# Retention and hard-swish MLP on one core: the heads' first values loaded as fp16 in 1 KB runs through GpSimd's queue and put in order by TensorE

## Chip, cores and metric

The kernel runs on one core of a Trainium2 chip. The metric is device time in microseconds, the median of several executions. A core has TensorE (PE, matrix products; PEld is its weight load), VectorE (DVE), ScalarE (ACT), GpSimd (POOL) and SyncE (SP). PE writes only to PSUM; the other engines take results from there back to SBUF. Transfers are issued by SP, ACT or POOL and run on 16 DMA engines that all three share. A transfer that changes the type on its way (fp32 to fp16) is issued from POOL here.

## The reference

Retention over 8 batches, 8 heads, 576 positions and a head dimension of 64, then a two-layer MLP on the 4608 tokens:

```python
scores = scale * np.matmul(q, k.transpose(0, 1, 3, 2))       # scale = 1/8
gamma = 1.0 - 2.0 ** (-5.0 - np.arange(H))                   # one decay per head
Dmat = np.where(rel >= 0, gamma[:, None, None] ** rel, 0.0)  # rel = row - column
attn = np.matmul(scores * Dmat, v)                           # (8, 8, 576, 64)
x = attn.transpose(0, 2, 1, 3).reshape(4608, 512)
h = x @ w_in                                                 # 512 -> 2048
out = (h * np.clip(h + 3.0, 0.0, 6.0) / 6.0) @ w_out         # 2048 -> 512
```

All inputs and the output are fp32. The products run in fp16 with sums in fp32.

## The kernel before, in words

**Blocks.** Each batch's 576 positions are cut into 64 first positions (the "heads" of the sequences, TL = 64) and one block of 512. The eight groups of 64 together make block 0, the eight blocks of 512 are blocks 1 to 8. Block 0 is computed directly, without a carried state; blocks 1 to 8 go in chunks of 128 positions that carry a state from chunk to chunk. For each block the MLP runs in two stages: 16 `up` units (`up_steps`, each four products of 128x512, then an ACT and a DVE instruction), and the `down` products. `down` of a block is interleaved with `up` of the next by plans written out by hand (`go`, and the tables behind it). The order on every engine is the order in which the program names the instructions.

**The start, on which the change works** (from `indices()` on, L714 to L784). For each of four pairs of heads (i = 0 to 3) the kernel loads k and q of the first 64 positions with `load_half`: 128 partitions hold (batch, r), each with 4 neighbouring positions times 64 values, so that each run in memory is 1 KB. Pair 0 of k goes by SP and ACT, all q by SP and ACT; k of pairs 1 to 3 goes by POOL, cast to fp16 on the way. `turn_heads` turns them with products against `by_chunk`, a permuted identity, so that the positions come out in order. `scores_heads` makes the scores, DVE multiplies them with a mask (L458). `inner_heads(i)` multiplies the masked scores with the values `vh` of pair i and writes a quarter of `xT0`, the input of the first `up` units. `idle_products` are products whose results nobody reads.

**The values of block 0.** `load_values` (L431, called twice) loads them by SP behind all of q, 128 partitions by position in the chunk, in runs of 64 values (256 bytes), fp32, into `vf`. `values_heads(c)` (L438) casts chunk c to fp16 into `vh`; ACT does chunks 0 and 1, POOL chunks 2 and 3. Each chunk holds all heads, so `inner_heads(0)` needs all four.

**The weights.** `win_piece(n)` (L642) loads a quarter of w_in (1 MB in fp32) as fp16 by POOL's queue; piece 0 goes in two halves, behind the last q (`queries`); pieces 2 and 3 and the four `wout_piece` (L650) are named after the first four units (L773 to L775), so that on POOL they stand behind its two casts of the values. Units 4n to 4n+3 use piece n. `decays()` (L120, POOL, then one ACT Exp) and two smaller tables stand on POOL behind the weights. `fetch(8, wout[2])` (L779) makes SP wait until the third w_out transfer has landed, and then loads the chunks of block 1.

**Queues.** A queue has eight semaphores for its transfers, used in turn, and in the built program a transfer that takes a semaphore again first waits, on the issuing engine, for the transfer that had it, eight before.

**Buffers.** PSUM tiles of tag `pp` have six buffers and take scores, `inner_heads` and `up` results in turn; tag `st` has two and takes the results of `turn_heads` and later of `down`. `ws[1]` to `ws[4]` hold sums of w_out later, and lend their space to early tables.

Of the kernel before, what the change touches and what calls it, by code (L numbers as in the profile page):

```python
# [12 lines left out]
FP32 = mybir.dt.float32  # L13
# [8 lines left out]
def kernel(  # L22
# [9 lines left out]
    nc = tc.nc  # L32
# [3 lines left out]
    P = 128  # L36
# [353 lines left out]
    def load_half(i, nm, e, queue, behind=None):  # L390

        if nm not in hd.setdefault(i, {}):
            if queue is nc.gpsimd:
                hd[i][nm] = heads16(i, nm)
            else:
                f = half_tile(io, "fq", i, FP32, "hq", bufs=2) if nm == "q" else io.tile(
                    [P, H * D], FP32, tag=f"f{nm}", name=f"h{nm}{i}")
                hd[i][nm] = f.rearrange("p (e j d) -> p e j d", e=2, j=NJ)
        d = queue.dma_start(hd[i][nm][:, e].rearrange("p j d -> p (j d)"),  # L399
                            dict(q=q, k=k, v=v)[nm][:, 2 * i + e, 0:TL, :].rearrange("b (r j) d -> r b (j d)", j=NJ))  # L400
        if behind is not None:
            after(d, behind)
        return d
# [6 lines left out]
    def cast_heads(i, nm, copy):  # L410
        t = heads16(i, nm)
        copy(t, hd[i][nm])
        hd[i][nm] = t

    def turn_heads(i, nm, copy):
        pt = psum.tile([P, NJ, P], FP32, tag="st", bufs=2, name=f"hpt{nm}{i}")
        for j in range(NJ):
            for e in range(2):
                nc.tensor.matmul(pt[e * D:e * D + D, j, :], hd[i][nm][:, e, j, :], by_chunk, start=True, stop=True,
                                 skip_group_check=True)  # L420
        t = half_tile(work, "qT", i, FP16, "hqT", bufs=3) if nm == "q" else work.tile(
            [P, H * D], FP16, tag="kT", bufs=4, name=f"hkT{i}")
        if nm == "q":
            copy(t.rearrange("p (x j r) -> p x j r", j=NJ, r=RP), pt.rearrange("p j (x r) -> p x j r", r=RP))
        else:
            copy(t.rearrange("p (x r j) -> p x r j", j=NJ, r=RP), pt.rearrange("p j (x r) -> p x r j", r=RP))
        hd[i][nm + "T"] = t.rearrange("p (c y) -> p c y", c=NCB)

    vf = gp.tile([P, NCB, H * D], FP32, tag="g", bufs=4, name="hv")

    def load_values(c, n):  # L431

        for e in range(2):
            b = c + NCB * e
            nc.sync.dma_start(vf[rows(e), c:c + n].rearrange("p c (h d) -> p (c h) d", h=H),  # L435
                              v[b:b + n, :, 0:TL, :].rearrange("b h s d -> s (b h) d"))

    def values_heads(c, copy):  # L438
        copy(vh[:, c].rearrange("p i e d -> p (i e d)"), vf[:, c])

    def keys_heads(i):
        pk = psum.tile([P, NCB, 2, D], FP32, tag="pp", name=f"hpk{i}")
# [199 lines left out]
    def win_piece(n, parts=1, behind=None):  # L642
        a, b = pieces_in[n]
        for i in range(parts):
            cc = slice(NP // parts * i, NP // parts * (i + 1))
            d = nc.gpsimd.dma_start(win16[n][:, cc], win_v[:, cc, BLK * a:BLK * b])
            if behind is not None:
                after(d, behind)
# [62 lines left out]
    with tc.manual_schedule(engines={ENG.PE, ENG.DVE, ENG.Pool, ENG.Activation, ENG.SP}):  # L711
        sp, act, pool = nc.sync, nc.scalar, nc.gpsimd
        on_act, on_dve = nc.scalar.copy, nc.vector.tensor_copy
        indices()  # L714
        for nm in ("k", "q"):
            landed = load_half(0, nm, 0, sp)
            keys = landed if nm == "k" else keys
            load_half(0, nm, 1, act)
        nc.scalar.activation(warm, half, ACTF.Exp)
        load_half(1, "q", 0, sp)  # L720
        load_half(1, "q", 1, act)
        for i in (2, 3):
            for e in range(2):
                queries = load_half(i, "q", e, sp, keys)
        load_values(0, 2)
        load_values(2, 2)
        for i in (1, 2, 3):
            for e in range(2):
                load_half(i, "k", e, pool, None if i == 1 else keys)
        win_piece(0, 2, queries)  # L730
        win_piece(1)
        distances()
        idle_products(5)
        mask_of_heads(0)
        cast_heads(0, "k", on_dve)
        turn_heads(0, "k", on_act)
        mask_of_heads(1)
        idle_products(4)
        cast_heads(0, "q", on_dve)
        mask_of_heads(2)  # L740
        turn_heads(0, "q", on_act)
        cast_heads(1, "q", on_dve)
        turn_heads(1, "k", on_act)
        turn_heads(1, "q", on_act)
        cast_heads(2, "q", on_dve)
        scores_heads(0)
        mask_of_heads(3)
        idle_products(1)
        turn_heads(2, "k", on_act)
        turn_heads(2, "q", on_act)  # L750
        cast_heads(3, "q", on_dve)
        scores_heads(1)
        idle_products(1)
        turn_heads(3, "k", on_act)
        turn_heads(3, "q", on_act)
        scores_heads(2)
        scores_heads(3)
        for c in range(NCB):
            values_heads(c, on_act if c < 2 else pool.tensor_copy)
        idle_products(2)  # L760
        inner_heads(0, on_act)
        inner_heads(1, on_act)
        inner_heads(2, on_dve)
        first = [up_steps(0, u) for u in range(4)]
        for dmc in range(3):
            for unit in first:
                next(unit)
            if dmc == 1:
                inner_heads(3, on_act)
        for unit in first:  # L770
            for _ in unit:
                pass
        for n in (2, 3):  # L773
            win_piece(n)
        wout = [wout_piece(pc) for pc in (0, 2, 1, 3)]  # L775
        decays()
        mask_of_chunk()
        decays_of_chunk()
        fetch(8, wout[2])  # L779
        for u in range(4, NFC):  # L780
            up_unit(0, u)
        weight_sums(3)
        weight_sums(1, 2, 4)
        down = down_plain(0)  # L784
        go("k0 D4 k1 D4 +1 k2 D4 +1 k3 D6 h0 D2 c4 h1 D3 h2 D3 h3 D3 D4 c5 t4 D5 a4 s4 u4 D5 z4 t5 c6 D4 "
           "x4 a5 s5 i4 u5 z5 D5 t6 x5 D2 i5 D4 L2 c7 a6 s6 u6 L3 z6 D1 t7 L3 x6 a7 s7 i6 u7 D1 L1 z7 L2 c8 L1 D2 x7 D1 i7 t8 D3 "
           "R3 c9 R3 a8 s8 u8 R2 t9 z8 R4 c10 x8 a9 s9 i8 u9 U1 z9 c11 t10 U3",
           1, down)
        down = down_plain(1)
        go("c12 D6 x9 a10 s10 i9 u10 z10 D2 t11 c13 +1 D7 x10 a11 s11 i10 u11 z11 c14 +2 D8 x11 D2 i11 t12 +1 D3 +1 D3 "  # L790
           "a12 s12 u12 t13 D2 c15 D2 z12 +1 D4 x12 a13 s13 i12 u13 z13 D1",
           down=down)
        go("U1 D3 t14 U1 D2 U1 U1 D2 x13 a14 s14 i13 u14 z14 o1 c16 U1 D2 U1 D2 t15 U1 D2 U1 D2 +1 U1 x14 a15 s15 i14 u15 z15 "
           "c17 D2 U1 D2 +1 U1 D2 +1 U1 D2 x15 +1 U1 i15 t16 c18 +1 U1 D2 t17 U1 U1",
           2, down)
        for kb in range(2, NB):
# [60 lines left out]
```

## Time and profile before

| | |
|---|---|
| three runs | 302.41, 302.86 (median), 303.16 us |
| profiled execution: span from first to last instruction | 301.3 us |
| between that span and the median of the runs | 1.56 us |
| PE busy, DVE, ACT, POOL | 95%, 70%, 64%, 42% of the span |
| DMA | 48.37 MB, mean 161 GB/s |

The profiled execution is one execution taken by the hardware's profiler. Only its span is listed, not a time of its own; what lies around the span is taken to be the 1.56 us between it and the median. In the profile a line is an engine, a source line of the kernel (L153 is the helper of all the 128-row products), the operation and the tiles' names. "x16" is a count. Where an idle time is given in brackets, it lies just ahead of the instruction, with what ended it. Start times are counted from the start of the span.

### The profile page before, as it was taken

What the parts mean: (1) busy time and instruction counts of PE and PEld (TensorE: products, weight loads), DVE (VectorE), ACT (ScalarE), POOL (GpSimd) and SP (SyncE); (2) the same over time, 40 slices, a digit from 0 to 9 for tenths busy, and PEclk for the clock granted to TensorE, in tenths of its full rate; (3) what the DMA queues carried; (4) which work ended last, traced back from release to release, by engine and by line L of the source; (5) the groups of instructions that cost most, each with busy time, mean ns of one, the idle gap of its engine ahead of it and who ended that gap; (6) DMA issues with size and microseconds to landing.
All of it is one profiled execution on the core that took longest, in us unless ns stands there. A gap on an engine that the chain in (4) does not pass through costs nothing.

```text
span 301.3 us, 12401 instructions
## 1 busy us (share of the span) xinstructions
PE 287.0 (95%) x5450; PEld 220.7 (73%) x5450; DVE 211.8 (70%) x382; ACT 193.8 (64%) x360; POOL 128.0 (42%) x163
## 2 busy tenths in 40 slices
PE   6839999989999999999999999999999999999995
PEld 2527866778655657888887877887878977787895
DVE  4713854678886777888968696779768776657554
ACT  5715875799876786866767667657766675555420
POOL 5247028553773750808641964195238003100510
PEclk9978999999999999999999999999999999999999
DMA  6999999998999989998999999979928100210114
GB/s 151 204 153 200 214 215 217 214 227 194 175 200 156 244 183 200 193 198 238 207 246 178 196 200 216 182 140 269 136 25 143 72 2 2 104 40 2 72 72 139
DMA packets 122549, 48.37 MB, mean 161 GB/s; under 512 B 96384, under 2 KB 117888, under 8 KB 122496
## 3 DMA queue, kind: packets, MB, share of 16 engines
q1 hardware_dynamic: 118496, 42.61, 72.0%
q0 software_dynamic: 3568, 4.59, 9.0%
q8 instruction: 42, 0.69, 1.0%
q10 hardware_dynamic: 432, 0.39, 0.4%
q14 instruction: 11, 0.09, 0.2%
HBM read 36.70 MB, written 9.44 MB: 153 GB/s over the span
## 4 chain that ended last, share of the span: by engine, by line
PE 89%; DMA 5%; ACT 2%; SPq 1%; DVE 1%; issue 0%; POOL 0%; ACTq 0%; POOLq 0%
PE ph L153 42%; PE pm L153 29%; PE pd L153 9%; PE po L231 4%; DMA hv<-in_v_dram 3%; PE pa L231 3%; DMA hq<-in_q_dram 2%; PE pu L231 1%; SPq L435 1%; PE ptk L153 1%; PE ptq L153 1%; SPq L399 1%; PE hpo L467 0%; ACT u L498 0%; DVE qT L211 0%; DVE g L500 0%
## 5 line engine op out<-in xcount | busy, mean ns | idle before, releaser
L153 PE MATMUL ph<-xT,win 128*64 128x512 f16 (+1 forms) x1248 | 146.3, 367 | 0.7 <-ACT xT L369 0.4
L500 DVE SCALAR_TENSOR_TENSOR g<-u,ph 128x512 f16<-128x512 f32 (+1 forms) x156 | 98.6, 644 | 53.4 <-ACT u L498 52.8
L498 ACT ACTIVATE u<-ph,half 128x512 f32<-128x512 f32 (+1 forms) x156 | 100.1, 659 | 42.6 <-PE ph L153 40.2
L153 PEld LDWEIGHTS <-win 128*64 128x64 f16 x1248 | 85.8, 136 | 26.1 <-issue 2.0
L153 PEld LDWEIGHTS <-g 128*64 128x64 f16 x928 | 51.7, 110 | 14.4 <-issue 0.4
L153 PEld LDWEIGHTS <-s 128*64 128x64 f16 x896 | 50.3, 110 | 8.3 <-issue 0.5
L317 POOL TENSOR_TENSOR z<-z,gpow 128x256 f32<-128x256 f32 x24 | 15.8, 657 | 70.6 <-DVE z L316 49.6
L153 PE MATMUL pm<-ws,s 128*64 128x256 f16 x672 | 45.7, 273 | 0.0
L192 POOL TENSOR_TENSOR q<-fq,dec 128x512 f16<-128x512 f32 x32 | 36.7, 1167 | 0.0
L369 ACT CAST xT<-po 128x256 f16<-128x256 f32 (+1 forms) x44 | 22.5, 583 | 21.5 <-PE po L231 21.5
L195 POOL TENSOR_TENSOR v<-fv,dec 128x512 f16<-128x512 f32 x32 | 35.4, 1111 | 1.9 <-DMA fv<-in_v_dram 1.9
L153 PE MATMUL pd<-wout,g 128*64 128x512 f16 x256 | 34.9, 382 | 0.1
L579 POOL TENSOR_TENSOR u<-u,p 128x512 f32<-128x512 f32 x7 | 8.9, 1271 | 60.4 <-ACT u L619 54.1
L153 PE MATMUL pm<-wout,g 128*64 128x256 f16 x448 | 31.1, 273 | 0.0
L266 DVE TENSOR_TENSOR a<-pa,mask 128x256 f16<-128x256 f32 (+1 forms) x44 | 21.9, 540 | 7.9 <-PE pa L231 4.2
L188 ACT CAST k<-fk 128x512 f16<-128x512 f32 x32 | 19.8, 620 | 0.0
L515 DVE TENSOR_TENSOR s<-g 128x1024 f16<-128x1024 f16 x28 | 19.3, 691 | 0.2
L323 ACT CAST z<-z 128x512 f16<-128x512 f32 x24 | 14.8, 619 | 5.2 <-DVE z L313 5.0
L153 PE MATMUL pm<-ws,g 128*64 128x256 f16 x224 | 16.7, 274 | 0.0
L153 PE MATMUL pm<-wout,s 128*64 128x256 f16 x224 | 16.3, 273 | 0.1
L515 DVE TENSOR_TENSOR s<-g,s 128x1024 f16<-128x1024 f16 x14 | 13.1, 934 | 0.0
L231 PE MATMUL po<-qT,z 64*64 64x64 f16 x512 | 12.5, 198 | 0.4 <-ACT z L326 0.3
(101 smaller groups left out, 252.6 us busy)
## 6 DMA issues: line engine op xcount, KB each, us to landing
fk<-in_k_dram SPq DMA_DIRECT2D x32, 256.0 KB, 4.6
fq<-in_q_dram SPq DMA_DIRECT2D x16, 512.0 KB, 6.1
fv<-in_v_dram SPq DMA_DIRECT2D x32, 256.0 KB, 5.9
out_dram<-o SPq DMA_DIRECT2D x14, 512.0 KB, 4.0
wout<-in_moe_w_out_dram POOLq DMA_DIRECT2D x4, 512.0 KB, 12.8
out_dram<-o SPq DMA_DIRECT2D x7, 256.0 KB, 5.1
win<-in_moe_w_in_dram POOLq DMA_DIRECT2D x3, 512.0 KB, 7.4
hv<-in_v_dram SPq DMA_DIRECT2D x4, 256.0 KB, 7.1
```

Of the source, the lines that this page charges most:

```text
L153: nc.tensor.matmul(out[r], lhs[:, r], rhs, skip_group_check=True, **flags)
L188: nc.scalar.copy(by_head(k16), in_rows(st[c]["fk"]))
L192: nc.gpsimd.tensor_tensor(by_head(q16[:, e]), in_rows(st[c]["fq"][:, :, e, :]), in_rows(dd[:, 2 + e, 0:H, :]), ALU.mult)
L195: nc.gpsimd.tensor_tensor(v16, st[c]["fv"], dd[:, 1, H:2 * H, :], ALU.mult)
L231: return lambda: nc.tensor.matmul(*args, skip_group_check=True, **flags)
L266: nc.vector.tensor_tensor(a16[:, a, 0:n].rearrange("p x i q -> p (x i) q"), pa[a].rearrange("p x i q -> p (x i) q"), m, ALU.mult)
L317: nc.gpsimd.tensor_tensor(new, new, decay, ALU.mult)
L323: nc.scalar.copy(z16, zs[c])
L369: nc.scalar.copy(xt[:, s], po[s].rearrange("p x n (e r) -> p x n e r", e=2))
L498: nc.scalar.activation(uu[:, 0:n], ph[:, 0:n], ACTF.Relu, bias=half, scale=1.0 / 6.0)
L500: nc.vector.scalar_tensor_tensor(out=g[:, hf, ths, jr, :], in0=by_half(uu), scalar=1.0, in1=by_half(ph), op0=ALU.min, op1=ALU.mult)
L515: nc.vector.tensor_tensor(*pend.popleft())
```

## The change

1. `load_values(i)` now loads the values of pair i by POOL's queue (L439 of the kernel after), cast to fp16 on the way, in the layout of q and k: two transfers of 128 partitions x 256 elements for each pair, 1 KB runs. The fp32 tile `vf` and its four SP transfers are gone.
2. `picks()`: four selection matrices in `pick` (the space of `ws[2]`), set to zero by POOL (128x2048 fp16, between k of pair 1 and k of pair 2) and filled by four DVE copies of `by_chunk` behind the first cast of k.
3. `values_heads(i)` now is 16 products on PE (four chunks x four j), 32 matmuls of 128 columns, and one copy from PSUM to `vh`: ACT for pairs 0, 1 and 3, DVE for pair 2. The four calls stand between `scores_heads(2)` and `inner_heads(2)`.
4. All weights are issued by POOL right behind the values, in the order w_in 0 to 3, w_out 0, 2, 1, 3. The wait for `queries` is gone.
5. `inner_heads(1)` is copied out by DVE instead of ACT. Two idle products (four matmuls) behind the scores are gone.

```diff
-    vf = gp.tile([P, NCB, H * D], FP32, tag="g", bufs=4, name="hv")
-    def load_values(c, n):
-        for e in range(2):
-            b = c + NCB * e
-            nc.sync.dma_start(vf[rows(e), c:c + n].rearrange("p c (h d) -> p (c h) d", h=H),
-                              v[b:b + n, :, 0:TL, :].rearrange("b h s d -> s (b h) d"))
-    def values_heads(c, copy):
-        copy(vh[:, c].rearrange("p i e d -> p (i e d)"), vf[:, c])
+    pick = ws[2].rearrange("p j n -> p (j n)").rearrange("p (j c m) -> p j c m", j=NJ, c=NCB)
+    def picks():
+        for j in range(NJ):
+            nc.vector.tensor_copy(pick[:, j].rearrange("p c (x j) -> p (c x) j", j=NJ)[:, :, j], by_chunk)
+    def load_values(i, behind=None):
+        t = heads16(i, "v")
+        for e in range(2):
+            d = nc.gpsimd.dma_start(t[:, e].rearrange("p j d -> p (j d)"),
+                                    v[:, 2 * i + e, 0:TL, :].rearrange("b (r j) d -> r b (j d)", j=NJ))
...
+    def values_heads(i, copy):
+        pv = psum.tile([P, NCB, 2, D], FP32, tag="st", bufs=2, name=f"hpv{i}")
+        for c in range(NCB):
+            for j in range(NJ):
+                product(pv[:, c], pick[:, j, c, :], hd[i]["v"][:, :, j, :], start=(j == 0), stop=(j == NJ - 1))
+        copy(vh[:, :, i], pv)
...
-        load_values(0, 2)
-        load_values(2, 2)
         for i in (1, 2, 3):
             for e in range(2):
                 load_half(i, "k", e, pool, None if i == 1 else keys)
-        win_piece(0, 2, queries)
-        win_piece(1)
+            if i == 1:
+                nc.gpsimd.memset(pick, 0.0)
+        for i in range(NP):
+            load_values(i)
+        win_piece(0, 2)
+        for n in (1, 2, 3):
+            win_piece(n)
+        wout = [wout_piece(pc) for pc in (0, 2, 1, 3)]
...
         cast_heads(0, "k", on_dve)
+        picks()
...
         scores_heads(2)
+        values_heads(0, on_act)
         scores_heads(3)
-        for c in range(NCB):
-            values_heads(c, on_act if c < 2 else pool.tensor_copy)
-        idle_products(2)
+        values_heads(1, on_act)
         inner_heads(0, on_act)
-        inner_heads(1, on_act)
+        values_heads(2, on_dve)
+        inner_heads(1, on_dve)
+        values_heads(3, on_act)
         inner_heads(2, on_dve)
...
-        for n in (2, 3):
-            win_piece(n)
-        wout = [wout_piece(pc) for pc in (0, 2, 1, 3)]
         decays()
```

More of the change, by code (lines that the diff above doesn't have):

```diff
@@ L427, in turn_heads @@
         hd[i][nm + "T"] = t.rearrange("p (c y) -> p c y", c=NCB)
-    vf = gp.tile([P, NCB, H * D], FP32, tag="g", bufs=4, name="hv")
-    def load_values(c, n):
-        for e in range(2):
-            b = c + NCB * e
-            nc.sync.dma_start(vf[rows(e), c:c + n].rearrange("p c (h d) -> p (c h) d", h=H),
-                              v[b:b + n, :, 0:TL, :].rearrange("b h s d -> s (b h) d"))
-    def values_heads(c, copy):
-        copy(vh[:, c].rearrange("p i e d -> p (i e d)"), vf[:, c])
+    pick = ws[2].rearrange("p j n -> p (j n)").rearrange("p (j c m) -> p j c m", j=NJ, c=NCB)
[4 more added lines that the diff above has]
+        t = heads16(i, "v")
+        for e in range(2):
+            d = nc.gpsimd.dma_start(t[:, e].rearrange("p j d -> p (j d)"),
+                                    v[:, 2 * i + e, 0:TL, :].rearrange("b (r j) d -> r b (j d)", j=NJ))
+            if behind is not None:
+                after(d, behind)
+        hd.setdefault(i, {})["v"] = t
+    def values_heads(i, copy):
[4 more added lines that the diff above has]
+        copy(vh[:, :, i], pv)
     def keys_heads(i):
@@ L723 @@
             for e in range(2):
-                queries = load_half(i, "q", e, sp, keys)
-        load_values(0, 2)
-        load_values(2, 2)
+                load_half(i, "q", e, sp, keys)
         for i in (1, 2, 3):
```

## The prediction

> **What bounds the kernel now.** I read the page first: its busy row and the chain that ended last.
>
> ```profile
> span 301.3 us, 12401 instructions
> PE 287.0 (95%) x5450; PEld 220.7 (73%) x5450; DVE 211.8 (70%) x382; ACT 193.8 (64%) x360; POOL 128.0 (42%) x163
> PE 89%; DMA 5%; ACT 2%; SPq 1%; DVE 1%; issue 0%; POOL 0%; ACTq 0%; POOLq 0%
> ```
>
> PE sets the end, so time is won only where PE stands or runs slowly. Next I looked for such places: PE's own waits after 20 us, and the chain in order of time at the start.
>
> ```profile
> PE ph L153 <- ACT xT L369: 0.4, 1, 0.4
> ```
> ```profile
> 10.73 8.68 DMA hv<-in_v_dram
> ...
> 19.54 1.18 POOL ws L439 x2
> 20.76 1.17 PE hpo L467 x18
> 21.93 3.43 PE ph L153 x16
> 25.36 0.22 PE hpo L467 x8
> 25.59 12.12 PE ph L153 x112
> 37.70 0.22 PE hpk L153 x8
> ```
>
> After 20.8 us no wait of PE is longer than 0.4 us. Before that the chain hangs on the last load of the values, issued at 10.73 and landed after 8.68 us, and on POOL's casts. In PE's timeline, with ACT's last copy of the scores' inputs:
>
> ```profile
> 12.65 0.40 PE L455 MATMUL hpa<-hqT,hkT 64*128 64x128 f16 x8
> 12.98 0.59 ACT L424 CAST hqT<-hptq 128x512 f16<-128x512 f32 x1
> 20.20 0.32 PE L467 MATMUL hpo<-ha,ws 128*64 128x128 f16 x2 [4.93 <-POOL ws L439]
> ```
>
> PE stands for 4.93 us ahead of 20.20. The stand costs twice, as the windows show (the number behind POOL is the granted clock):
>
> ```profile
> 22.00:24.00 2.00, 2.00 (x12) 1.04 (x10) 0.66 (x1) 0.19 (x1) 2.00 (x5) 0.50 0.85 112
> 26.00:28.00 2.00, 2.00 (x22) 1.65 (x19) 0.55 (x1) 1.48 (x4) 1.75 (x11) 1.00 1.26 211
> ```
>
> After the stand the clock is 0.50, and 1.00 again only by 26 us: the first 8 products (16 matmuls) of `up` take 3.43 us, while the next 56 take 12.12, or 0.216 each. At that pace the 8 take 1.73.
>
> **When the values land now.** In the built program every POOL transfer from the ninth on waits for the one eight before it. POOL's issue times, from its timeline, and landings, from narrow windows of the DMA view (last number: us from issue to landing; first and last k transfer of the queue, then w_in piece 0's first half, piece 1 and piece 2):
>
> ```profile
> 4.26 2.07 POOL L399 DMA_DIRECT2D hk<-in_k_dram  x4 [1.21 <-DMA hk<-in_k_dram]
> 11.26 2.22 POOL L646 DMA_DIRECT2D win<-in_moe_w_in_dram  x3 [4.92 <-DMA hq<-in_q_dram]
> 20.65 1.48 POOL L646 DMA_DIRECT2D win<-in_moe_w_in_dram  x2
> 22.12 2.15 POOL L651 DMA_DIRECT2D wout<-in_moe_w_out_dram  x4
> ```
> ```profile
> hk<-in_k_dram POOLq DMA_DIRECT2D x1, 64.0 KB, 5.1
> hk<-in_k_dram POOLq DMA_DIRECT2D x1, 64.0 KB, 4.9
> win<-in_moe_w_in_dram POOLq DMA_DIRECT2D x1, 256.0 KB, 6.7
> win<-in_moe_w_in_dram POOLq DMA_DIRECT2D x1, 512.0 KB, 9.8
> win<-in_moe_w_in_dram POOLq DMA_DIRECT2D x1, 512.0 KB, 5.6
> ```
> ```profile
> masks.py:197 POOL MEMSET ident<- 128x128 f16 x1 | 0.2, 194 | 0.0
> L439 POOL CAST ws<-hv 128x512 f16<-128x512 f32 x2 | 1.2, 606 | 6.1 <-DMA hv<-in_v_dram 6.1
> L841 POOL MEMSET const-float32-0.0<- 128x1 f32 x1 | 0.1, 103 | 0.3 <-issue 0.3
> ```
>
> The new memset of 2048 elements is not in the trace. From 103 ns for one element and 194 for 128 it is 0.1 + 2047 x 0.72 ns = 1.6 us; by the cast's 1.18 ns per element, 2.4. I take 1.8, nearer the row of its own kind. It begins when the first two k issues are done (about 3.05), ends at 4.85, and puts the next k transfers 0.6 us later: the last is issued at 6.4 and lands at 11.3. PE takes it up at 11.86 today, and DVE casts its first q at 7.16:
>
> ```profile
> 11.86 0.44 PEld L419 LDWEIGHTS <-hk 128*64 128x64 f16 x8
> ```
> ```profile
> 7.16 0.43 DVE L412 CAST hq<-hq 128x512 f16<-128x512 f32 x1 [2.66 <-DMA hq<-in_q_dram]
> ```
>
> So the delay is hidden; with a memset of 2.4 us it just is.
>
> Each 64 KB issue takes 2.07 / 4 = 0.52 us. Values of pair 0 go out at 6.95 and 7.5, pair 1 at 8.0 and 8.6; pairs 2 and 3 wait for the k transfers, which land 4.9 after their issue, and go out at 9.8, 10.3, 10.8 and 11.3. For the DMA time, packets in 2 us of only 1 KB packets, and in 1 us of only 256-byte ones:
>
> ```profile
> DMA packets 693, 0.46 MB, mean 229 GB/s; under 512 B 80, under 2 KB 693, under 8 KB 693
> DMA packets 748, 0.19 MB, mean 189 GB/s; under 512 B 748, under 2 KB 748, under 8 KB 748
> ```
>
> 16 engines x 2 us / 693 is 46 ns a packet; 16 / 748 is 21. The values' 4096 short packets cost 5.5 us of all engines, the 1024 long ones (with 128 for semaphores) 3.3. In the queue behind k (11.3) the eight transfers land about 0.36 apart: pair 0 at 12.0, 1 at 12.7, 2 at 13.4, 3 at 14.1. The last needs 2.8 from its issue, what the first k transfer of all, on idle engines, took:
>
> ```profile
> hk<-in_k_dram ACTq DMA_DIRECT2D x1, 128.0 KB, 2.8
> ```
>
> **What PE does with them.** A group of 4 products of 128 columns takes 0.22 (the row of L153 hpk); `values_heads` has 16 products, 0.88 us; scores and `inner_heads` 0.22 each. From 12.65: scores 2 to 12.87; values 0 to 13.75; scores 3 to 13.97 (ACT's copy is ready at 13.57); values 1 to 14.85; inner 0 to 15.07; values 2 to 15.95; inner 1 to 16.17; values 3 to 17.05; inner 2 to 17.27. The copies lie beside it: 0.59 us on ACT by the row above, and DVE has 1.1 us for its own, from 15.95 to 17.05; each has at least another product group between it and its user, as have the copies to xT. So pairs 0 to 3 are needed at 12.87, 13.97, 15.07 and 16.17, and land 0.9 to 2.1 earlier. The picks are four DVE copies of 128x128, 0.27 us each by the same copy in `indices`:
>
> ```profile
> L104 DVE COPY by_chunk<-ident 128x128 f16<-128x128 f16 x1 | 0.3, 266 | 0.0
> ```
>
> 1.1 us after 4.85, over ahead of DVE's cast at 7.16. They are hidden; if the memset ended after 6.1, that cast and the first scores would wait. The dropped idle products are replaced by real ones, so the clock stays.
>
> **The weights.** w_in's first half waits for the first values: issue 11.85, 0.6 later than today. In an empty queue a piece lands after 5.6; the pieces then follow each other by (36.87 - 26.25) / 4 = 2.65 us, from piece 2's landing (20.65 + 5.6) to the time at which SP, which waits for the third w_out (L779), goes on:
>
> ```profile
> 36.87 0.42 SPq L174 DMA_DIRECT2D fk<-in_k_dram  x1
> ```
>
> From 14.1 on: pieces 0 to 3 by 16.75, 19.4, 22.05, 24.7, w_out by 27.4, 30.0, 32.7, 35.3. Needed: 17.27 (first half), then every four units, 3.46 us, from 20.95 on; w_out from 31.3. All are there. POOL is through with its issues at about 17.9, and with `decays`, 16 operations of 0.196 us by their row, at 21; ACT comes to the Exp, behind the fourth unit, at about 23.
>
> ```profile
> L123 POOL TENSOR_SCALAR arg<-fj 128x4 f32<-128x4 f32 x8 | 1.6, 196 | 0.3
> ```
>
> If POOL ran over 2 us later, ACT would hold the next units.
>
> **Sum.** The block of 56 products begins at 17.27 + 1.73 + 0.22 = 19.22 instead of 25.59: 6.37 us gained, 4.66 from the stand and 1.71 from the clock. Against it stands the supply of block 1. SP goes on at 32.7, only 4.2 earlier, so relative to PE the chunks come 2.2 late. Today's first q chunk and what hangs on it:
>
> ```profile
> fq<-in_q_dram SPq DMA_DIRECT2D x1, 512.0 KB, 6.1
> ```
> ```profile
> 43.91 2.04 POOL L192 TENSOR_TENSOR q<-fq,dec 128x512 f16<-128x512 f32 x2
> ```
> ```profile
> 47.25 0.56 PE L153 MATMUL ptq<-ident,q 128*64 128x128 f16 x14
> ```
>
> POOL's products end at 45.95, 1.3 ahead of PE. Of the 2.2 this cover takes 1.3; 0.9 is left, with ends 0 (POOL was waiting for other work) and 2.2. I take 0.9, from these rows. Gain 5.5: the span is 295.8, and with the 1.56 around it 297.4, which is 0.982 of the median.
>
> **A rule against it.** DVE's casts of q lie among POOL's issues (0.43 us each), and POOL's k issues kept 0.52 us. The Trainium skill (SBUF — State Buffer, the "DVE blocks DMA" trap) says that descriptors of a GpSimd transfer cannot be written while DVE runs a two-port copy, and that such a DMA took some 3100 instead of 620 ns. By it the values come later; no run here shows it, and it is the third rival.
>
> **The rivals.**
>
> 1. *w_in comes as late as today* (issue to landing 6.7, 8.0 and 9.8 although the short packets are gone). Then piece 0 lands at 18.55 and 20.6, piece 1 at 23.15; PE loses 1.4 at the third product step and 0.8 at unit 4. Gain 6.37 - 2.2 = 4.2: 298.7. Against it: the 5.6 in an empty queue. 12%.
> 2. *PE's clock falls or comes late*, because k is later by 0.6 or some values make PE stand: one clock interval as long as today's, 3.43 us at half speed, costs 1.7, and with the 0.9 the gain is 3.8: 299.1. Against it: PE has work on all of 12.65 to 19.2. 8%.
> 3. *DVE holds up POOL's issues* by all its copies between 4.5 and 12 us, 4 x 0.27 and 4 x 0.43: 2.8 us on everything in that queue. SP then goes on at 35.5, 1.4 earlier than today, with 1.3 of cover: gain 2.7, 300.2. This is the mechanism of the rule above. 9%.
> 4. *Slower: the values wait in POOL's queue.* If pair 0 lands after PE has stood long enough to lose its clock, PE has 6.35 us of work from there to the block of 56, some 2.2 more at the low clock. Today's 25.59 is reached when pair 0 lands at 25.59 - 8.6 = 17.0, 10 us after its issue; that is the point. At 19.4, where hv lands today, it costs 2.4: 305.3. Against it: k in this queue needed 4.9 and 5.1, beside q. 8%.
> 5. *Nothing is gained*, because the supply of later chunks takes all back: 302.9. Against it: SP goes on at least 4 us earlier, and fewer packets are moved. 3%.
>
> **How the numbers follow.** The forecast has 60%, with its own range 296.4 (no loss to the chunks) to 298.2. The range goes from 296.0 to 300.2 and takes in rivals 1 to 3; it leaves out 4 and 5. About 0.3%, 0.9 us, is what a measurement can tell here. Faster: 60 + 12 + 8 + 9 = 89%; same 3%; slower 8%.
>
> **What would show it.** In the profile after: POOL's memset 1.6 to 2.4 us; pair 0 to 3 landed by 12.0 to 14.1; 128 matmuls of 128 columns at 28 ns apart; no PE wait over 1 us between 12.6 and 20; clock 1.00 in all windows to 30 us; the 56-product block at 19.2; SP going on at 32 to 33; a wait of about 1 us at PE's first q turn. A PE stand at `values_heads` would make rivals 3 or 4 right, one at the first `up` units rival 1, matmuls 56 ns apart rival 2. The forecast is wrong if a value load lands 2 us later than listed.

## The result, and the profile after

The changed kernel takes 300.80 us (median of 12 runs, 299.96 to 302.71) against 302.76 (12 runs) of the kernel before on the same chip. The ratio is 0.9944, 95% interval 0.9921 to 0.9968: faster by 0.56%, 2.0 us, where 5.5 were forecast and 296.0 to 300.2 was the range. The span of the profiled execution went from 301.3 to 299.3 us. From the page of the kernel after, its span and the chain that ended last by engine:

```profile
span 299.3 us, 12661 instructions
PE 79%; DMA 9%; POOL 6%; SPq 2%; ACT 2%; issue 1%; DVE 1%; POOLq 0%; ACTq 0%
```

DMA and POOL now hold 15% of the chain, where PE alone held 89% before. First the place at which the change was aimed, PE's timeline (start, duration, idle time ahead in brackets):

```profile
12.93 1.08 PE L153 MATMUL hpv<-hv,ws 128*64 128x128 f16 x32
14.28 1.08 PE L153 MATMUL hpv<-hv,ws 128*64 128x128 f16 x32
15.42 1.06 PE L153 MATMUL hpv<-hv,ws 128*64 128x128 f16 x32
16.53 1.06 PE L153 MATMUL hpv<-hv,ws 128*64 128x128 f16 x32
18.06 1.95 PE L153 MATMUL ph<-xT,win 128*64 128x512 f16 x16 [0.25 <-DMA win<-in_moe_w_in_dram]
20.07 1.93 PE L153 MATMUL ph<-xT,win 128*64 128x512 f16 x16
22.27 1.08 PE L153 MATMUL ph<-xT,win 128*64 128x512 f16 x8 [0.28 <-DMA win<-in_moe_w_in_dram]
```

The stand of 4.93 us is gone, no group of the new products waits for a value, and the first 16 matmuls of `up` take 1.95 us instead of 3.61 (the same row before): the clock stays up. The block of 56 products begins at 20.07 instead of 25.40, 5.33 earlier. What waits now is `up`, for w_in. POOL's issues, and how long the transfers needed from issue to landing (last number; the last value, w_in's first half, second half and piece 1, w_out's first piece):

```profile
6.94 4.87 POOL L439 DMA_DIRECT2D hv<-in_v_dram  x8
11.65 3.84 POOL L658 DMA_DIRECT2D win<-in_moe_w_in_dram  x5
15.30 1.80 POOL L663 DMA_DIRECT2D wout<-in_moe_w_out_dram  x3
```
```profile
hv<-in_v_dram POOLq DMA_DIRECT2D x1, 64.0 KB, 3.2
win<-in_moe_w_in_dram POOLq DMA_DIRECT2D x1, 256.0 KB, 6.4
win<-in_moe_w_in_dram POOLq DMA_DIRECT2D x1, 256.0 KB, 6.9
win<-in_moe_w_in_dram POOLq DMA_DIRECT2D x1, 512.0 KB, 9.1
wout<-in_moe_w_out_dram POOLq DMA_DIRECT2D x1, 512.0 KB, 15.0
```

The issues began at 11.15, 11.65, 12.38, 13.09 and 15.30. So the last value lands at 14.4, the two halves of piece 0 at 18.0 and 19.3, piece 1 at 22.2, w_out's first at 30.3. The windows show the transfers at that time (last three numbers: granted clock, DMA share, GB/s):

```profile
12.00:14.00 2.00, 1.93 (x57) 1.58 (x53) 2.00 (x5) 1.28 (x3) 2.00 (x4) 1.00 1.06 125
14.00:16.00 2.00, 2.00 (x72) 1.90 (x72) 1.74 (x3) 1.18 (x3) 2.00 (x5) 1.00 0.80 96
16.00:18.00 2.00, 1.82 (x66) 1.65 (x60) 1.43 (x3) 0.84 (x2) 1.10 (x3) 1.00 1.05 160
18.00:20.00 2.00, 1.94 (x22) 1.31 (x24) 0.55 (x1) 0.22 (x1) 1.37 (x6) 1.00 1.24 208
```

From 18 us on the engines move 208 GB/s. From 14 to 18, where the first of w_in comes, they move 96 and 160: 2 x (112 + 48) = 320 KB are missing, 1.5 us at 208 GB/s. By the landings it is more: piece 0 is complete 4.9 us behind the last value, where 2.65 were reckoned, 2.3 too many. With the 0.3 us by which the last value is late (14.4, forecast 14.1) that makes up the 2.5 us by which the third w_out, and with it SP, is later than forecast. The chain and the waits show what follows:

```profile
16.36 18.84 DMA wout<-in_moe_w_out_dram
35.22 0.41 SPq L174
42.20 7.00 DMA fq<-in_q_dram
```
```profile
PE ptq L153 <- POOL q L192: 1.7, 3, 0.6
PE ph L153 <- DMA win<-in_moe_w_in_dram: 0.5, 2, 0.3
```

SP goes on at 35.22, only 1.65 earlier than before, while PE is 4.8 ahead (`hpk` at 32.69 instead of 37.49). PE then waits for q of block 1: for its first chunk, and for the second, which was issued at 42.20 and took 7.0 us to land. To see where the gain goes I set DVE's 44 mask products of the chunks (L266) against those of the kernel before, the first with the first and so on. Gain in us, with the time at which SP goes on:

| kernel | SP on | block of 56 | 49.5 us | 58 us | end of span |
|---|---|---|---|---|---|
| after | 35.22 | 5.33 | 4.04 | 2.45 | 2.0 |
| gate one piece earlier | 33.40 | 4.53 | 3.53 | 3.53 | 2.7 |
| memset on DVE | 34.24 | 4.46 | 4.47 | 3.90 | 3.0 |
| three alterations | 31.04 | 6.47 | 6.05 | 4.79 | 3.9 |
| before + idle products | 35.44 | 1.93 | 1.95 | 1.95 | 0.2 |

The lower rows are kernels of the experiments. In the kernel after 2.9 us are lost between 20 and 58 us, nearly all to supply.

Each row rests on one profile, and the start of a kernel is not the same in each. Four kernels of the last experiment (long runs, no loads) have the instructions of these two up to some 60 us, and so show the start again. In the kernel before, PE's stand at the values was 4.93 us; in two such profiles it is 2.58 and 4.70:

```profile
18.04 0.32 PE L477 MATMUL hpo<-ha,ws 128*64 128x128 f16 x2 [2.58 <-POOL ws L449]
19.88 0.32 PE L473 MATMUL hpo<-ha,ws 128*64 128x128 f16 x2 [4.70 <-POOL ws L445]
```

At 58 us the first is 2.36 us ahead of the profile used here, the second 0.24 behind it. The changed kernel has its block of 56 at 20.07, 21.12 and 20.66 in three profiles, and a gain of 2.45, 3.14 and 3.56 at 58 us. So differences of this size between two rows of the table can be chance. What all three profiles of the changed kernel have in common is the late supply: piece 0 complete at 19.3, 19.9 and 19.9, the third w_out at 35.2, 36.0 and 35.2 where 32.7 was forecast.

### The profile page after: what moved, and what is told of

It is laid out like the page before. It is cut to its first block, busy times and chain, and to the rows that moved or that the text cites. A ratio compares the mean times of both kernels' runs of the same rounds, so it can differ in the third digit from the quotient of the medians.

```text
span 299.3 us, 12661 instructions
## 1 busy us (share of the span) xinstructions
PE 287.4 (96%) x5574; PEld 219.3 (73%) x5574; DVE 216.2 (72%) x388; ACT 193.9 (65%) x360; POOL 133.7 (45%) x170
## 4 chain that ended last, share of the span: by engine, by line
PE 79%; DMA 9%; POOL 6%; SPq 2%; ACT 2%; issue 1%; DVE 1%; POOLq 0%; ACTq 0%
PE ph L153 37%; PE pm L153 29%; DMA wout<-in_moe_w_out_dram 6%; PE pd L153 5%; PE po L231 4%; DMA fq<-in_q_dram 2%; PE pa L231 2%; SPq L174 2%; POOL hv L439 1%; POOL hk L399 1%; POOL win L658 1%; PE pu L231 1%; POOL ws L741 1%; PE ptk L153 1%; POOL q L192 1%
## 5 line engine op out<-in xcount | busy, mean ns | idle before, releaser
L153 PE MATMUL ph<-xT,win 128*64 128x512 f16 (+1 forms) x1248 | 144.8, 364 | 1.2 <-DMA win<-in_moe_w_in_dram 0.5
L153 PEld LDWEIGHTS <-win 128*64 128x64 f16 x1248 | 82.9, 136 | 28.6 <-DMA win<-in_moe_w_in_dram 1.1
L153 PEld LDWEIGHTS <-g 128*64 128x64 f16 x928 | 51.1, 110 | 14.9 <-issue 0.4
L266 DVE TENSOR_TENSOR a<-pa,mask 128x256 f16<-128x256 f32 (+1 forms) x44 | 21.9, 539 | 8.4 <-PE pa L231 4.7
L188 ACT CAST k<-fk 128x512 f16<-128x512 f32 x32 | 19.9, 622 | 2.1 <-DMA fk<-in_k_dram 2.1
L527 DVE TENSOR_TENSOR s<-g 128x1024 f16<-128x1024 f16 x28 | 19.3, 692 | 0.2
L153 PE MATMUL pm<-ws,g 128*64 128x256 f16 x224 | 16.7, 274 | 0.0
## 6 DMA issues: line engine op xcount, KB each, us to landing
wout<-in_moe_w_out_dram POOLq DMA_DIRECT2D x4, 512.0 KB, 17.9
```

The lines of the kernel that those rows point to most:

```text
L153: nc.tensor.matmul(out[r], lhs[:, r], rhs, skip_group_check=True, **flags)
L188: nc.scalar.copy(by_head(k16), in_rows(st[c]["fk"]))
L266: nc.vector.tensor_tensor(a16[:, a, 0:n].rearrange("p x i q -> p (x i) q"), pa[a].rearrange("p x i q -> p (x i) q"), m, ALU.mult)
L527: nc.vector.tensor_tensor(*pend.popleft())
```

## The experiments

**Theory A:** what is missing went to the late arrival of the weights, and through SP's gate (L779 before, 794 after) to the chunks of block 1. **Rivals:** DVE's copies hold up POOL's descriptors (B); w_in's first reading is slow by itself (C); the weights alone, or the clock alone, made the gain. Each ratio below is to the kernel before, run beside it on the same chip (medians there 302.35, 302.37, 302.57, 302.36).

### The gate one piece earlier

```diff
-        fetch(8, wout[2])
+        fetch(8, wout[1])
```

> The kernel after, but SP goes on to block 1's chunks when the second w_out transfer has landed instead of the third. Theory (the wait of SP sets when the chunks come, and the DMA engines are half empty while SP starts up behind it): SP goes on at about 32.9 instead of 35.2, PE's waits for the q products of chunks 4 and 6 (1.7 us) go down to 0.5 or less, time 1.0 to 1.5 us under the kernel after's 300.8. Rival (the bytes are the bound, not the wait): the third and fourth w_out come as much later as the chunks come earlier, PE stands for them in the first down products, time 300.5 to 301.5.

300.21 us, ratio 0.9904 (0.9872 to 0.9935). SP goes on at 33.40, no wait for `ptq` is left, and nothing is lost between 49.5 and 58 us; in the kernel after 1.6 were. This fits that the late chunks took the gain there. PE waits 0.8 us for w_in at 23.6 us, ten ahead of the gate, so not by its doing: piece 1 landed at 23.55 in this profile, 22.2 in the kernel after. The median is 0.6 under the kernel after, less than the 1.0 to 1.5 expected, and the intervals of the two ratios overlap.

### The weights alone

```diff
         win_piece(0, 2, queries)
-        win_piece(1)
+        for n in (1, 2, 3):
+            win_piece(n)
+        wout = [wout_piece(pc) for pc in (0, 2, 1, 3)]
-            values_heads(c, on_act if c < 2 else pool.tensor_copy)
+            values_heads(c, on_act if c < 2 else on_dve)
```

This is the kernel before; the later issues of w_in and w_out are deleted from their old place.

> The kernel before with one part of the change alone: all weights are issued by POOL in one go behind w_in 0 (which still waits for q); the values come by SP in 256-byte runs as before, chunks 2 and 3 are cast by DVE instead of POOL so that POOL waits for nothing. Theory (PE's start behind the values sets the time, the weights were early enough): values still land near 19.4, the long block of up products begins at about 25.2 instead of 25.6, SP goes on at about 34.5 instead of 36.9, time 302.3. Rival (the supply behind the weights is the bound by itself): 301 or less, as SP goes on 2.4 us earlier.

302.05 us, ratio 0.9997 (0.9964 to 1.003): nothing, though SP goes on at 34.88. The values still come late (17.8 in this profile) and the first 16 matmuls of `up` still take 3.63. The weights alone did not make the gain.

### DVE without the mask of block 0

```diff
-            nc.vector.tensor_tensor(a16[:, h2], pa[h2], m, ALU.mult)
+            pass
```

`inner_heads` multiplies with `by_chunk` in its place.

> The kernel after without block 0's multiplication of the scores with the mask (DVE leaves it out, the inner products take a constant matrix instead of the masked scores), so that DVE is idle from 12 to 16 us. Rival B (DVE's work holds up the descriptors of POOL's transfers): the first half of w_in lands by 16 instead of 18.05, SP goes on at about 33.3, time 299.3. Rival C (the first reads of w_in are slow by themselves) and the theory that POOL's pace sets it: landing at 18.0 +- 0.3, SP at 35.2 +- 0.4, time within 0.4 of 300.8.

300.02 us, ratio 0.9927 (0.9896 to 0.9957). DVE has nothing to do from 12 to 16 us, and w_in's start is as slow as before:

```profile
14.00:16.00 2.00, 2.00 (x72) 1.80 (x68) 0.00 (x0) 0.79 (x2) 2.00 (x5) 1.00 0.78 97
16.00:18.00 2.00, 2.00 (x80) 2.00 (x74) 1.08 (x2) 0.87 (x2) 1.24 (x3) 1.00 0.90 138
```

97 and 138 GB/s, with DVE at 0.00 in the first row. Rival B falls for this stretch. The median is 0.8 under the kernel after, where 0.4 at most was expected; the intervals overlap, and nothing here explains it.

### w_in touched ahead

```diff
+        touch = const.tile([P, NP, 8], FP32, name="touch")
+        nc.sync.dma_start(touch, win_v[:, :, 0:8])
```

A small transfer by SP behind q reads 32 bytes of each row of w_in's first columns.

> The kernel after with one more transfer on SP behind q: 32 bytes of each row of w_in, read by nobody. Rival C (the first reads of w_in are slow by themselves, whatever the queue): w_in's first packets run at full rate from the start, the first half lands by 16.3 instead of 18.05, SP goes on at about 33.5, time 299.5. Rival B (descriptors held up by DVE) and the theory of POOL's pace: no change, 18.0 +- 0.4, SP at 35.2 to 35.8, time 300.8 to 301.2, as the 512 short packets cost 0.6 us of the DMA engines.

299.82 us, ratio 0.9901 (0.9868 to 0.9935). From 14 to 18 us the engines move 121 and 168 GB/s instead of 96 and 160: a little better, not 208. SP goes on at 35.33, no earlier, and still no wait for q is left in its profile: its q chunks landed 4.5 to 5.1 us after their issue, in place of 5.4 to 7.0 in the kernel after. C is true in part at the most, and what brought q earlier here isn't shown.

### The memset on DVE

```diff
-                nc.gpsimd.memset(pick, 0.0)
+                nc.vector.memset(pick, 0.0)
```

> The changed kernel with the zeroing of the pick matrices on DVE instead of POOL (POOL's memset took 1.84 us at 3.02, and two 128x128 operations of DVE beside it took 2.69 and 2.56 us). Theory A (what is lost is the arrival of the weights, and with it SP's going on at 35.2): everything behind the memset in POOL's queue is issued some 1.8 us earlier, w_in's first half lands near 16.3 instead of 18.05, SP goes on near 33.5, PE's waits for q in block 1 (2.9 us in all) shrink by about 1.5, and the time is 299.0 to 299.6, 1.2 to 1.8 below the changed kernel. The two DVE operations go back to about 0.3 us. Rival R (w_in's slow start is over at a fixed time, near 18, however early it is asked for): issues earlier, but SP still goes on at 34.5 to 35.5 and the time stays at 300.5 to 301.

300.10 us, ratio 0.9914 (0.9874 to 0.9954). From DVE's timeline of this kernel, and ahead of it from that of the kernel after:

```profile
2.25 2.69 DVE L110 TENSOR_SCALAR early<-query,fj 128x128 f32<-128x128 f32 x1
2.45 2.56 DVE L111 TENSOR_SCALAR early<-query,last 128x128 f32<-128x128 f32 x1
```
```profile
2.43 0.91 DVE L741 MEMSET ws<- 128x1024 uint32 x1 [0.16 <-issue]
3.33 0.28 DVE L110 TENSOR_SCALAR early<-query,fj 128x128 f32<-128x128 f32 x1
```

DVE needs 0.91 us for what took POOL 1.84. POOL's queue gains nothing by it: the values' issues now wait for the k transfers, and w_in is asked for at 11.79, no earlier than in the kernel after (11.65). So the expectation's premise failed, and rival R was not put to the test. Yet w_in's start is better, 156, 171 and 201 GB/s in the windows from 14, 16 and 18 us instead of 96, 160 and 208, and its first half lands at 16.9. It does so, at 16.6 and 16.7, in the two other kernels with this memset (three alterations, below), against 17.9 to 18.6 in the six profiles with POOL's memset and the same order of issues. What the memset has to do with it isn't shown. SP goes on at 34.24, 1.0 earlier and not 1.8, and the waits for q are gone. Against A's 299.0 to 299.6 the time is 0.5 too long: in the profiled execution TensorE came to full clock only at 14.2 us, and lost 0.9 us on its first products.

### w_in ahead of the values

```diff
+        win_piece(0, 2)
         for i in range(NP):
             load_values(i)
-        win_piece(0, 2)
```

> The changed kernel with w_in's first piece issued ahead of the values instead of behind them. If the slow start belongs to the first reading of w_in itself, it passes while the values are still being loaded: the first piece lands by about 14 to 15, the later pieces run at 2.65 us each, SP goes on at 32.5 to 33.5, the values land 1.5 to 2.5 us later, so that PE stands 0.5 to 1.5 us at them, and the time is 299.5 to 300.5. If it belongs to the queue at that time (about 12 to 18 us), the first piece moves at 100 to 160 GB/s still, the values behind it land after 17, PE stands 3 us or more at them, and the time is 302 or more.

301.84 us, ratio 0.9969 (0.9941 to 0.9998): 1.0 slower than the kernel after. Neither number came out. w_in is slow at 10 to 12 us now, when it is first read (114 GB/s). POOL's timeline and PE's wait show what that does to the values:

```profile
14.33 0.51 POOL L439 DMA_DIRECT2D hv<-in_v_dram  x1 [1.66 <-DMA win<-in_moe_w_in_dram]
15.69 0.51 POOL L439 DMA_DIRECT2D hv<-in_v_dram  x1 [0.85 <-DMA win<-in_moe_w_in_dram]
```
```profile
PE hpv L153 <- DMA hv<-in_v_dram: 2.9, 1, 2.9
```

The last two value transfers wait on POOL until w_in's two halves have landed. PE stands 2.9 us and loses its clock (0.50 in the window from 18 us). When w_in's later pieces begin, near 17.5, the windows from 18 and 20 us have 165 and 200 GB/s: the slow start is shorter the second time. This speaks for C, that the first reading is what is slow; why it is slow no run shows.

### The clock alone

```diff
         for c in range(NCB):
+            if i == 0 and c == 2:
+                for _ in range(22):
+                    product(spare[0], ident16, ident16.unsqueeze(1).to_broadcast([P, NP, P]), start=True, stop=True)
             for h2 in range(2):
```

This is the kernel before, with 22 idle products in `inner_heads(0)`, where PE stands for the values (`spare[0]` is the PSUM tile of the idle products).

> The kernel before with 22 more idle products of 512 columns (0.21 us each) where TensorE stands for the values (15.3 to 20.2 us); nothing else is changed, so that only the clock term of the change is tried. If the clock term is right: the 18 products of 128 columns at 20.8 and the 16 of 512 at 21.75 (3.61 us) run at full speed, the block of 56 products begins 1.6 to 1.8 us earlier (23.6 to 23.8); SP still goes on at 36.9, so of the 1.7 us some 0.4 go at block 1's q (cover 1.3), and the time is 301.2 to 301.7. Rival: the low clock is a matter of time and not of the stand: the products stay at 56 ns per 128 columns, and the time is 302.8 as before.

302.66 us, ratio 1.0018 (0.9988 to 1.0049): no gain in the whole time. But the mechanism is there. PE's timeline:

```profile
20.51 0.72 PE L472 MATMUL hpo<-ha,ws 128*64 128x128 f16 x20
21.47 1.95 PE L153 MATMUL ph<-xT,win 128*64 128x512 f16 x16 [0.23 <-ACT xT L474]
23.47 4.88 PE L153 MATMUL ph<-xT,win 128*64 128x512 f16 x42
139.78 0.40 PE L231 MATMUL po<-a,v 64*64 64x64 f16 x25 [0.99 <-issue]
```

16 matmuls in 1.95 instead of 3.61, and the block 1.93 earlier: 1.66 from the clock on these 16, the rest because the products ahead of them began 0.25 earlier (the values landed at 18.0 in this profile, 19.4 in the kernel before). 1.95 stand until 125 us; then PE loses 1.8 in three stands that no instruction and no load of the profile ends. The waits of this kernel behind 60 us have one row for the two longest:

```profile
PE po L231 <- issue: 1.5, 2, 1.0
```

The page lists one more queue, of instructions, with packets of 16 KB:

```profile
q8 instruction: 43, 0.70, 1.0%
```

In the trace of this kernel packets of q8 end near 138.4, 182.6 and 213.6 us, and the three stands near 139.8, 184.0 and 214.9, each 1.3 to 1.4 us later. Over all traces of this study PE's starts lie more than 0.45 us apart 27 times between 112 and 285 us (in the kernels before and after never), and each of the 27 ends 1.24 to 1.54 us behind a packet of q8, which come about every 6.5 us.

### Values by SP, all weights first

```diff
-            d = nc.gpsimd.dma_start(t[:, e].rearrange("p j d -> p (j d)"),
+            d = nc.sync.dma_start(f[:, e].rearrange("p j d -> p (j d)"),
```

`f` is an fp32 tile, and DVE casts it (`cast_heads(i, "v", on_dve)`, four times).

> The changed kernel with the values loaded by SP behind q, in the same runs of 1 KB but as fp32, cast by DVE (four casts of 128x512, 0.43 us each), and all weights directly behind the keys in POOL's queue (4.9 us of POOL's issues gone ahead of them). Theory A (the arrival of the weights sets what was lost): w_in is asked for at 6.9 instead of 11.65, SP goes on at 31 to 33, PE's waits for q in block 1 are gone, and the time is 298 to 299. Rival S (the DMA engines are shared): q and the values come later beside w_in, TensorE starts its scores later than 12.7 or stands at the values by 1 us or more, and what block 1 gains is given back: 300 to 301.5.

306.29 us, ratio 1.0105 (1.0062 to 1.0148): slower than before. SP goes on at 33.34, but PE stands:

```profile
PE hpv L153 <- DVE hv L412: 2.7, 3, 1.5
```

Rival S, and worse than it said: the stands cost the clock (0.50 from 18 to 20 us), as forecast rival 4 had it for another cause. The profiled execution, 303.92, is the shortest of the six; what the longer ones lost has no profile. Here the values had to come ahead of the weights.

### Three alterations together

```diff
-                nc.gpsimd.memset(pick, 0.0)
+                nc.vector.memset(pick, 0.0)
-        idle_products(5)
+        idle_products(7)
-        idle_products(4)
+        idle_products(6)
-        fetch(8, wout[2])
+        fetch(8, wout[1])
```

> The changed kernel with three small alterations: the pick matrices are zeroed by DVE, SP's chunks wait for the second w_out piece in place of the third, and 4 more idle products of 512 columns (2 behind the first 5, 2 behind the next 4) fill TensorE's gaps of 0.7 and 0.6 us before 8 us. Theory: SP goes on near 32, no wait for q stands in block 1, TensorE comes to full clock by 10 us at the latest instead of 14.2 (as it was with the memset on DVE), and the block of 56 products begins at 19.8 to 20.3: 298.5 to 299.5. Rival: the supply was no longer on the path with the memset on DVE, and the clock rises when it will: 299.8 to 300.3, as with the memset alone.

299.36 us, ratio 0.9914 (0.9887 to 0.9941), the shortest median among the kernels that do the whole work. SP goes on at 31.04, TensorE is at full clock by 7.9, and the block of 56 begins at 18.93:

```profile
18.93 1.93 PE L153 MATMUL ph<-xT,win 128*64 128x512 f16 x16
```

Of the gain of 6.47 there, 3.9 are left at the end. By medians it is 3.2 us under before; the interval overlaps with those of its parts, so that no one of the three is shown to be worth its place. And though SP goes on 5.8 us earlier than in the kernel before, 1.3 are lost between 49.5 and 58 us: the second q chunk, issued at 40.39, took 6.5 us to land.

### Less load on the DMA engines, behind 85 us

Two sets of kernels ask whether the late stands come from the load. First, long runs: from chunk 12 on each partition reads 2 KB (k, v) or 4 KB (q) in one piece; for k and v:

```diff
+                if c < 12:
...
+                else:
+                    d = nc.sync.dma_start(t.rearrange("p h d -> p (h d)"),
+                                          src[b].rearrange("h s d -> (h s d)")[s0 * D * H:(s0 + P) * D * H].rearrange("(p x) -> p x", p=P))
```

> The kernel before with the chunks from 12 on loaded in long runs (2 or 4 KB for each partition, the same bytes, other rows of q, k and v in place of the right ones, so that the values of the output are others while every instruction of the engines stays). It takes the load off the DMA engines from some 85 us on (q1 moved 51481 packets there between 125 and 230 us, 96.7% of the engines). Reference for the two kernels below. If TensorE's late stands (waits put down to issue, 0.5 to 1.2 us each, 125 to 230 us) come from that load, they are rare here: 300.5 to 302.3. If they do not, the time is 302.3 to 302.8 as before.

> The kernel before with the 22 more idle products while TensorE stands for the values, and with the chunks from 12 on in long runs as in the kernel ahead (output values others for the same reason). Theory L (the clock term is real, and its 1.95 us at 125 us were lost again to stands of TensorE under the DMA load): 1.5 to 2.0 us below the kernel ahead, and no wait of TensorE put down to issue over 0.4 us between 125 and 230 us. Rival N (the gain is lost for another reason, such as supply of the chunks or the clock at the start): less than 0.7 us below it.

> The changed kernel with the chunks from 12 on in long runs (output values others for the same reason). Theory L: what the change gains by 60 us (2.45 in its profile) is what it gains at the end, 2.2 to 2.7 us below the kernel before with the same long runs; rival N: under 1.7 us below it.

303.89 (outside both numbers expected), 301.52 and 301.84 us (ratios 1.0049, 0.9979 and 0.9973; 1.0022 to 1.0076, 0.9957 to 1.0002, 0.9944 to 1.0002). Against the first the clock alone gains 2.4 and the change 2.05. The packets fell to less than half, the load only to 76%, and the stands stayed: three, one and two over 0.45 us. The longest, in the first and the third:

```profile
PE po L241 <- issue: 1.3, 1, 1.3
```
```profile
PE po L241 <- issue: 1.2, 1, 1.2
```

This was too little to tell. So, second, no loads at all from chunk 16 on:

```diff
+        if c >= 16:
+            st[c].update(kept_in)
+            return dmas
```

> The kernel before without the loads of the chunks from 16 on (blocks 5 to 8 work on the q, k and v of chunks 14 and 15 again, so that the output of those blocks is another; every instruction of TensorE, VectorE, ScalarE and GpSimd stays). If DMA load on the instruction queue makes TensorE's late stands: no wait put down to issue over 0.3 us behind 110 us, and the time is 300.8 to 302.2. Rival (the stands have nothing to do with the loads): stands of 0.5 us or more behind 110 us as in most of the kernels so far, 302.3 to 303.5.

> The kernel before with the 22 idle products and without the loads of the chunks from 16 on (output of blocks 5 to 8 another). If the clock term is real in the whole time and was lost only to the late stands: 1.4 to 2.2 us below the kernel before without those loads. Rival: within 0.6 us of it, as with the loads (302.66 against 302.37).

> The changed kernel without the loads of the chunks from 16 on (output of blocks 5 to 8 another). Theory: the gain by 60 us stays to the end, 2.0 to 3.2 us below the kernel before without those loads. Rival: under 1.7 us.

> The changed kernel with the memset on DVE, SP behind the second w_out piece, 4 more idle products, and without the loads of the chunks from 16 on (output of blocks 5 to 8 another). Theory: its profile's gain by 60 us, 4.8, stays to the end: 4.2 to 5.2 us below the kernel before without those loads. Rival: 3.2 or less, as with the loads (299.36 against 302.57).

301.88, 301.48, 298.77 and 299.88 us (ratios 0.9976, 0.9967, 0.9879 and 0.9896; 0.9949 to 1.0002, 0.9936 to 0.9999, 0.9841 to 0.9918, 0.9855 to 0.9938). q1 has some 40% of the engines between 125 and 230 us, in place of 97%. Three of the four profiles lose nothing of their gain between 118 and 242 us, the fourth 0.6; of the ten kernels with all loads the kernel after loses 0.2, the other nine 0.45 to 1.8. So with less load less of the gain is lost. That the load makes the stands is likely and not shown: over 0.45 us there are 18 in the eleven kernels with all loads (none in two of them, the kernels before and after), six in the three with long runs, three in these four. The changed kernel now gains 3.1 us against the first of the four (the intervals of the two don't meet), and in its profile the gain of 3.56 at 58 us is 4.04 at 242. The idle products gain 0.4, which is within the intervals: what the clock term is worth in the whole time stays open (no gain, 2.4 and 0.4 us in three comparisons). The fourth missed its expectation: its profiled span is 296.9, but its six runs spread from 298.28 to 300.35. What the longer ones lost has no profile.

## Why the prediction was wrong

**Right.** The values land from 11.1 to 14.4 us (12.0 to 14.1 forecast), and PE never stands for them; the four groups take 0.9 to 1.0 us each; the memset took 1.84 for 1.8; and the clock is 1.00 in all windows from 12 to 24 us, so that the term for the clock came in full. Rivals 2, 4 and 5 were wrong. The direction was right, and the size was not.

**The step that failed** is "From 14.1 on: pieces 0 to 3 by 16.75, 19.4, 22.05, 24.7, w_out by 27.4, 30.0, 32.7, 35.3." The distance of 2.65 us was right: measured are 19.3, 22.2, 24.75, 27.3, then 30.3, 32.75 and 35.2, 2.6 apart behind piece 1. What was wrong is that it held from the first packet on: piece 0 needed 4.9 us behind the last value. I took it from pieces 2 and on, and today's first pieces, 6.7 to 9.8 us from issue, were in the prediction's own rows; I put them down to the short packets beside them. Those are gone, and the first pieces still need 6.4, 6.9 and 9.1. That was rival 1, to which I gave 12%, if not in its full size (18.0, 19.3 and 22.2 where it had 18.55, 20.6 and 23.15); and I charged it to `up` alone and not to SP's gate.

**What follows from it**, in the terms of the sum. The block of 56: 6.37 forecast, 5.33 measured (1.0 less; 0.8 of it is `up` beginning at 18.06 instead of 17.27). From there to 33 us 0.5 more for w_in, forecast nothing. SP: 32.7 forecast, 35.22 measured, 2.5 later. The loss to block 1: 0.9 forecast, with 2.2 as its upper end; measured 4.8 - 2.45 = 2.35 between 33 and 58 us (1.1 and 0.7 in the two other profiles of the same instructions). Last, 0.45 behind 58 us, forecast nothing. 5.33 - 0.5 - 2.35 - 0.45 = 2.0. That the supply came 2.5 us late, and lost this at w_in's first piece, is shown by the landings. That the gate's lateness is what block 1 cost is argued: the kernels with the earlier gate and the memset on DVE, which move SP to 33.40 and 34.24, lose none and 0.6 there, but the one with w_in touched ahead loses none with SP at 35.33, and the one with three alterations 1.3 with SP at 31.04. The second q chunk's own time to landing enters too: 7.0 us in the kernel after, 5.6 with the earlier gate, 6.5 with three alterations.

**Mis-sized.** The cast packets of 1 KB took 60 ns in the middle, not 46: 46 was the engines' time by the count of all packets in a window. At 60 the values' 1024 packets need 3.8 us instead of 3.3. The values' issues took 0.61 each instead of 0.52; w_in was asked for at 11.65, near the 11.85 forecast. And the 4.66 us of gain from the stand came from one profile: the stand was 4.93 us in it, and 4.70 and 2.58 in the two others of the same instructions.

**Rival 3** came nearest in time, 300.2, and in SP's time, 35.5, by luck: its delay of 2.8 us on POOL's issues did not come, as w_in was asked for at 11.65. The kernel without the mask adds that DVE's mask products don't make w_in's start slow.

**Still open.** What makes w_in's first reading slow, and why it is less so with the memset on DVE; how much of the loss at block 1 is the gate's; what the clock term is worth by itself; and whether the gain of the kernel with three alterations comes from each of them.

## What to carry to other kernels

A pace read from the middle of a queue isn't the pace of its start: take the first transfer's time from issue to landing from the row of a first transfer. A stand read from one profile is one draw: here it was 4.93, 4.70 and 2.58 us in three of the same instructions. When the bound engine comes forward by some microseconds, ask of each load behind a gate whether the gate comes forward as far, and charge the difference to the place where that load is used. And a gain seen at 60 us of a profile is worth its face value only if nothing behind it is close to late: here stands of up to 1.3 us took some of it back, not the same in each kernel.

## What the runs showed of the hardware that was not expected

- **TensorE's late stands follow packets of the instruction queue.** Stands of up to 1.3 us, each ending 1.24 to 1.54 us behind a 16 KB packet of q8: 18 in nine kernels with q1 at 86 to 99% of the engines (none in the kernels before and after, at 97 and 99%), 3 in four kernels with it at some 40%. That the packet is what it waits for is read from these times; no run moved the packets themselves. The Trainium skill (Runtime: NRT & Kernel Launch, "Instruction fetch mechanics") describes such 16 KB blocks and calls the cost of crossing one mostly hidden. These runs agree with "mostly": a profile has 26 or 27 such packets between 112 and 285 us, and none to three of them are followed by a stand.
- **A memset of POOL stretches DVE.** Two operations of 128x128 took 2.69 and 2.56 us beside it, 0.28 without, and ended within 0.2 us of its end (4.86). The Trainium skill (SBUF — State Buffer, "Who interferes with whom") gives a port that the two engines lock against each other. The ends fit that; but the two operations began at 2.25 and 2.45, ahead of the memset's recorded start at 3.02, and that it is this lock isn't shown.
- **The rise of the clock was not fixed.** With the same starts of PE's first products it came to full speed at 9.7 us in the kernel after and at about 12 in the one with the earlier gate; with the gaps ahead of 8 us filled, by 7.9.
